# Attention rows stored a tile later, a PSUM bank of rows per engine, list entries made two tiles at a time, and another order behind the last tile

## The chip, the cores and the metric

The kernel runs on one core of a Trainium2 chip. The time is the device time of one execution in microseconds. Before the change it is 892.62 us, the median of 3 runs (892.03 to 894.59). The profile comes from one more execution.

## The reference

Three layers follow one another on 3072 tokens of 512 numbers (4 sequences of 768 steps, 8 heads of 64):

```python
for t in range(S):                       # linear attention with a decay per head
    state = gamma * state + k[t] (x) v[t]
    y[t] = scale * q[t] @ state
logits = x @ w_gate + modality_bias[modality_id]
e_idx  = argmax(logits); gate_w = softmax(logits)[e_idx]
out[e_idx == e] = gate_w * (relu(x @ w1[e]) @ w2[e])      # 8 experts, one for each token
return ((x @ mw1) * (x @ mw2)) @ mw3 @ w_out              # last layer, no activation behind w3
```

Since nothing nonlinear stands between `mw3` and `w_out`, the kernel multiplies these two matrices once ("the fold": 64 units of three 128x512 matmuls) and uses the product for all tokens. Several weights arrive as 64-bit floats, and are decoded on the chip with integer operations ("a decode").

## The kernel before, in words

**Attention.** The tokens go in 24 tiles of 128 (six for each sequence). One Python loop over t writes the program of all engines: in step t the scores of tile t+1 (`scores`, matmuls L331, masked copies on VectorE L333), the output rows of tile t-1 (`rows_gate`, L378), the list entries that are due (`entries`, L447), and tile t itself (`attend_T` L342, `attend_v` L350, `state` L366). Queries, keys and values come as one transposed tile `qkv` (loaded six tiles ahead, seven buffers), a second key tile `kT` (loaded three tiles ahead, four buffers) from tile 6 on; the first six are made on TensorE. Every engine runs its instructions in the order in which this loop writes them, and so do SP's DMA issues. A row tile goes to DRAM (`x_scratch`, L383) where it is made.

**Rows.** `rows_gate(t)` puts the output of a tile and its gate logits, head by head, into one PSUM tile `r` of two banks. ScalarE scales heads 0 to 3 (four instructions, L380), VectorE heads 4 to 7 (L381), and the logits of all heads (`Lh`, L382).

**Routing.** After every batch of tiles (`BATCHES`) VectorE reduces the logits, finds the best expert and its weight (`route_a`), TensorE counts places within experts (`route_mm`, L412 and L414), VectorE finishes (`route_b`). Then each tile gets an entry: VectorE makes a 128x128 one-hot matrix `oh` (L440), TensorE multiplies (L447), ScalarE copies the 16x128 result `ls` (L449), and GpSimd scatters it into a DRAM table `tok_scratch` (L450). The table is filled with a default value at the start (a store of 97x2x256 numbers, L580).

**The two queues.** Routing and entry steps wait in `rq`, decodes in `dq`; at the end of each step `spend(BUDGET)` writes about 2.5 us of VectorE steps from `rq` first, and then from `dq`. `LOAD_T` says after which tiles the loads of the first two 1-MB weights (`f64f`, L189) are written, `SPLIT_T` at which tiles a decode joins `dq`.

**Behind the last tile.** TensorE works off the 64 fold units in pieces (`fold_mm`, lengths in `FM`, matmuls L244, results stored by `fold_out` L261), between them the routing of the last batch, the last entries, the tables of counts, the reading of the lists (`lists_get`, GpSimd, L497), their transposition (`tables3`, L525), the gathers of tokens by list (L793), and the decodes of the last five weights (`fold_a`, `fold_b`). The first expert slot begins with the first matmul of L233 and all slots follow from there to the end.

Of the kernel before, what the change touches and what calls it, by code (L numbers as in the profile page):

```python
# [10 lines left out]
F32 = mybir.dt.float32  # L11
# [83 lines left out]
def pack(q, k, v, moe_modality_id, moe_w_gate, moe_modality_bias, moe_w1, moe_w2, moe2_w1, moe2_w2, moe2_w3, moe2_w_out):  # L95
# [29 lines left out]
    }  # L125
FM = [6, 6, 13, 12, 8, 8]


def kernel(tc, a, out):
# [3 lines left out]
    with ExitStack() as ctx:  # L133
# [45 lines left out]
        pad = ct([1, 1], F32, "pad")  # L179
        lists = fold.tile([P, 2, T2], F32, name="lists")  # L180

# [99 lines left out]
        L = pa.tile([P, NTILE, E], F32, name="L")  # L281
        Lh = pa.tile([P, NTILE, H, E], F32, name="Lh")
        OH = pa.tile([P, NTILE, 2, E], F32, name="OH")
        tmp.append(pa.tile([P, NTILE, E], F32, name="tmp2"))
        none = lists[:TRP]
        io = pa.tile([P, P], F32, name="io_sb")
# [84 lines left out]
        def rows_gate(t):  # L371
            s = st[t]
            xr = pa.tile([P, H, D], F32, tag="xr", name=f"xr{t}", bufs=3)
            b = psr.tile([P, 2, 512], F32, tag="r", name=f"r{t}")[:, :, :4 * HW].rearrange("p x (h w) -> p x h w", h=4)
            g = gx[:, t % NC]
            for hp in range(4):
                z = hp % 2 * 2
                nc.tensor.matmul(b[:, hp // 2, z:z + 2].rearrange("p h w -> p (h w)"), lhsT=s["xT"][:, hp, :], rhs=iwg[:, hp].rearrange("p z w -> p (z w)"), start=True, stop=True)  # L378
            for h in range(4):
                nc.scalar.activation(xr[:, h], b[:, 0, h, :D], AF.Copy, scale=g[:, h:h + 1])  # L380
            V.tensor_tensor(xr[:, 4:], b[:, 1, :, :D], bc(g[:, 4:].unsqueeze(2), [P, 4, D]), op=ALU.mult)  # L381
            V.tensor_tensor(Lh[:, t].rearrange("p (x h) e -> p x h e", x=2), b[:, :, :, D:], bc(g.rearrange("p (x h) -> p x h", x=2).unsqueeze(3), [P, 2, 4, E]), op=ALU.mult)  # L382
            nc.sync.dma_start(xd[t * P:t * P + P, :], xr.rearrange("p h d -> p (h d)"))  # L383
            del st[t]


        def route_a(t0, t1):
            sl, sh = slice(t0, t1), [P, t1 - t0, E]
            V.tensor_reduce(L[:, sl], Lh[:, sl].rearrange("p t h e -> p t e h"), axis=AX.X, op=ALU.add)
# [48 lines left out]
        def places(t):  # L438
            oh = pa.tile([P, P], F32, tag="oh", name=f"oh{t}", bufs=6)
            V.tensor_scalar(oh, io, rk[:, t], None, op0=ALU.is_equal)  # L440
            return oh

        def entries(ohs):
            b = bank()[:2 * E]
            for i, (t, oh) in enumerate(ohs):
                c = slice(i * P, i * P + P)
                nc.tensor.matmul(b[:, c], lhsT=OHV[:, t].rearrange("p z e -> p (z e)"), rhs=oh, start=True, stop=True)  # L447
                ls = pa.tile([2 * E, P], F32, tag="ls", name=f"ls{t}", bufs=4)
                nc.scalar.copy(ls, b[:, c])  # L449
                nc.gpsimd.indirect_dma_start(out=tbl.rearrange("r i -> (r i)").rearrange("(r w) -> r w", w=P), out_offset=bass.IndirectOffsetOnAxis(ap=gix[:, t:t + 1], axis=1), in_=ls, in_offset=None)  # L450

# [14 lines left out]
        gt = CV("gt").rearrange("p (a b) -> p a b", a=E)  # L466

        def tables0():
            c = CV("c16")[:E]
            V.tensor_scalar(nbt, CV("ones")[:E], base[:E, -1:], c, op0=ALU.mult, op1=ALU.subtract)  # L470
# [45 lines left out]
        def tables2b():  # L516
            b = bank()
            for x in range(5):
                nc.tensor.matmul(b[:1, x * CW:x * CW + CW], lhsT=c3[:, x:x + 1], rhs=ident[:, :CW], start=True, stop=True)
            V.tensor_copy(ctl[:, :5 * CW], b[:1, :5 * CW])  # L520

        def tables3():
            b = bank()
            for x in range(2):
                nc.tensor.transpose(b[:, x * P:x * P + P], lists[:, 0, x * P:x * P + P], ident)  # L525
            nc.sync.dma_start(lsd, lists[:NSLOT].rearrange("p z i -> p (z i)"))
            V.tensor_copy(gidx, b[:, :T2].rearrange("p (x j) -> p x j", x=2)[:, :, :NSLOT])

# [17 lines left out]
        nc.gpsimd.memset(Ts[1], 0.0)  # L546
        nc.gpsimd.memset(none[:, 0], float(NT))
        nc.gpsimd.memset(none[:, 1], 0.0)
        nc.gpsimd.memset(iwg[:, :, :, D:], 0.0)
# [81 lines left out]

        def listing(t):
            listed.append((t, places(t)))
            yield .24

# [12 lines left out]
        for t in range(-1, NTILE + 1):  # L648
            for x in {-1: (3, 4, 5)}.get(t, (t + QB - 1,)):
                if x < NTILE:  # L650
                    run(load(x))
            load_k(t + 3)
            if t == 0:
                late_loads()
            if 1 < t + 2 < NTILE and t >= 0:
                vprime(t + 2)
# [44 lines left out]
        def fold_a():  # L701
            if not todo:
                return
            cur.append(fold_split(todo[0], V))
            for _ in range(3):
                next(cur[0])
# [8 lines left out]


        t0, t1 = bounds[-2], bounds[-1]
        while rq:
            spend(99.)
        listed += [(t, places(t)) for t in pend]  # L720
        pend.clear()
        run(routed(t0, t1))
        settle_lists()
        for r in ready:
            route_exp(*r)
        ready.clear()
        fold_mm(FM[0])
        g = settled(t0, t1, route_mm(t0, t1))
        for _ in range(2):
            next(g)  # L730
        bn = tables0()
        finish()
# [642 lines left out]
```

## Time and profile before

| | us |
|---|---|
| median of 3 runs | 892.62 |
| the profiled execution | 891.8 |
| its span on the core | 890.0 |
| TensorE busy | 852.4 (96% of the span) |
| VectorE, ScalarE, GpSimd busy | 485.0, 313.6, 321.3 |
| start of the last rows' entry (L447, tile 16) | 141.16 |
| start of the first expert slot (L233) | 206.36 |

"Busy" counts the time in which an engine runs an instruction; the rest of the span is idle, and the profile names what ended each idle stretch. TensorE's granted clock is given as a share of 2.4 GHz: 1.00 is the upper of its two levels, 0.50 the lower. The share of the DMA is a mean over 16 DMA engines.

### The profile page before, as it was taken

To read this page: it belongs to the slowest core of one execution; us is meant where nothing else is said; L and a number is where in the kernel's file an instruction comes from. 1 tells how busy PE (TensorE), PEld (TensorE's weight loads), DVE (VectorE), ACT (ScalarE), POOL (GpSimd) and SP (SyncE) were. 2 spreads that over 40 slices of the span, in tenths; PEclk is the share of its full clock that TensorE was granted. 3 is DMA by queue.
4 is the path that set the end of the run, shared out by engine and by line. 5 is a ranking of instruction groups with operands and counts; after the bars stand their busy time and mean duration, and the time that the engine had idled before them with its cause. 6 is when DMAs were issued, how large, how long until landed. Compare 5 with 4: busy or idle time off the path is not lost. (4 is left out here: it accounts for less than half of the span.)

```text
span 890.0 us, 16627 instructions
## 1 busy us (share of the span) xinstructions
PE 852.4 (96%) x6363; PEld 770.8 (87%) x6363; DVE 485.0 (54%) x724; ACT 313.6 (35%) x618; POOL 321.3 (36%) x295
## 2 busy tenths in 40 slices
PE   9699997979999999999999998999999999999997
PEld 8598885659999999899999976887887887999997
DVE  2379885755251515661111554256226375999993
ACT  4254442225213131713121442233223253454551
POOL 3223342323003123632200215246326354755663
PEclk9799999999999999999999999999999999999999
DMA  7989842386443526772516019813111414644411
GB/s 276 357 295 315 322 169 85 115 326 217 188 144 144 184 101 204 257 278 93 170 49 253 11 54 386 322 60 142 60 59 48 155 48 154 220 169 145 155 48 60
DMA packets 59334, 152.11 MB, mean 171 GB/s; under 512 B 6775, under 2 KB 20229, under 8 KB 57689
## 3 DMA queue, kind: packets, MB, share of 16 engines
q1 hardware_dynamic: 51321, 127.19, 39.8%
q0 software_dynamic: 7904, 23.53, 7.2%
q8 instruction: 61, 1.00, 0.5%
q14 instruction: 48, 0.39, 0.1%
HBM read 100.98 MB, written 49.75 MB: 169 GB/s over the span
## 5 line engine op out<-in xcount | busy, mean ns | idle before, releaser
L233 PE MATMUL b<-h,wh 128*128 128x256 f32 x768 | 139.9, 284 | 1.1 <-ACT xh L807 1.1
L1007 PE MATMUL al<-xh,ws 128*128 128x512 f32 x384 | 125.4, 394 | 2.0 <-DMA ws<-ws_scratch 1.4
L233 PEld LDWEIGHTS b<-h,wh 128*128 128x128 f32 x768 | 119.7, 192 | 1.7 <-ACT xh L807 1.5
L917 DVE SCALAR_TENSOR_TENSOR h<-b,h 128x512 fp32r<-128x512 f32 x48 | 32.6, 689 | 157.7 <-ACT h L916 157.7
L233 PE MATMUL b<-xh,wl 128*128 128x256 f32 x384 | 108.7, 283 | 0.3 <-DVE wl L204 0.3
L233 PE MATMUL b<-xh,wh 128*128 128x256 f32 x384 | 108.8, 283 | 0.1
L233 PE MATMUL b<-xl,wh 128*128 128x256 f32 x384 | 108.6, 283 | 0.0
L233 PE MATMUL b<-h,wl 128*128 128x256 f32 x384 | 108.6, 283 | 0.0
L1007 PEld LDWEIGHTS al<-xh,ws 128*128 128x128 f32 x384 | 72.0, 188 | 19.5 <-issue 1.7
L1295 PE MATMUL oa<-wfh,ab 128*128 128x256 f32 x384 | 74.9, 284 | 0.7 <-DVE ot L1302 0.6
L1007 PE MATMUL al<-xl,ws 128*128 128x512 f32 x192 | 75.1, 391 | 0.0
L233 PEld LDWEIGHTS b<-xh,wl 128*128 128x128 f32 x384 | 73.7, 192 | 0.5 <-DVE wl L204 0.5
L233 PEld LDWEIGHTS b<-xh,wh 128*128 128x128 f32 x384 | 73.6, 192 | 0.4 <-issue 0.3
L233 PEld LDWEIGHTS b<-xl,wh 128*128 128x128 f32 x384 | 73.7, 192 | 0.0
L233 PEld LDWEIGHTS b<-h,wl 128*128 128x128 f32 x384 | 73.7, 192 | 0.0
L1007 PE MATMUL ga<-xh,ws 128*128 128x512 f32 x192 | 63.6, 392 | 2.3 <-ACT p L1120 1.8
L1295 PEld LDWEIGHTS oa<-wfh,ab 128*128 128x128 f32 x384 | 61.5, 189 | 2.6 <-DVE ot L1302 2.2
L916 ACT ACTIVATE h<-b 128x512 fp32r<-128x512 f32 x48 | 28.4, 597 | 85.2 <-PE b L233 83.7
L952 ACT COPY yT<-b 128x512 f32<-128x512 f32 x24 | 14.1, 588 | 118.5 <-PE b L233 118.5
L1295 PE MATMUL oa<-wfl,ab 128*128 128x256 f32 x192 | 53.8, 280 | 0.0
L204 POOL TENSOR_TENSOR wo<-dec,wo 128x512 fp32r<-128x512 f32 x12 | 16.6, 1394 | 99.2 <-ACT wo L203 99.2
L204 POOL TENSOR_TENSOR xl<-y,xh 128x1024 fp32r<-128x1024 f32 x9 | 21.8, 2425 | 78.5 <-ACT xh L203 78.4
(235 smaller groups left out, 1929.1 us busy)
## 6 DMA issues: line engine op xcount, KB each, us to landing
qkv<-in_qkv SPq DMA_DIRECT2D x22, 768.0 KB
ws_scratch<-wo SPq DMA_DIRECT2D x28, 512.0 KB
ws<-ws_scratch SPq DMA_DIRECT2D x28, 512.0 KB
raw<-in_wall SPq DMA_DIRECT2D x24, 512.0 KB
ab<-ab_scratch SPq DMA_DIRECT2D x24, 512.0 KB
f64f<-in_w SPq DMA_DIRECT2D x8, 1024.0 KB
f64m<-in_m SPq DMA_DIRECT2D x16, 512.0 KB
y_scratch<-yT SPq DMA_DIRECT2D x14, 512.0 KB
```

What stands on the lines that cost most here:

```text
L204: lo_eng.tensor_tensor(lo, src, hi.bitcast(F32), op=ALU.subtract)
L233: nc.tensor.matmul(b, lhsT=x, rhs=y, start=first and n == 0, stop=last and n == 3 * len(ks) - 1)
L916: nc.scalar.activation(h, b, AF.Relu)
L917: V.scalar_tensor_tensor(l, b, 0.0, h.bitcast(F32), op0=ALU.max, op1=ALU.subtract)
L952: nc.scalar.copy(yT[:, 2 * dp:2 * dp + 2, :].rearrange("p a t -> p (a t)"), b)
L1007: nc.tensor.matmul(b, lhsT=y, rhs=r[:, kk, :], start=first and n == 0, stop=n == 5, skip_group_check=True)
L1295: nc.tensor.matmul(b, lhsT=x[:, k], rhs=y[:, k], start=first and n == 0, stop=n == 11, skip_group_check=True)
```

## The change

1. *Stores.* The store of a tile's rows is collected in `stores` and issued by `store_rows()` in the next step, behind that step's loads.
2. *Loads.* `kT` is loaded four tiles ahead into five buffers. The 1-MB loads and the decodes of the loop stand at other tiles. The table's fill is two stores of 97x256.
3. *Rows.* `r` becomes two PSUM tiles, `r0` for ScalarE, `r1` for VectorE. The logits are multiplied in two instructions, the second (heads 0 to 3) written behind `attend_v`. `Lh` keeps two batches.
4. *Entries.* Two tiles at a time: two one-hot matrices, two matmuls, one copy; up to three behind the last tile. The scatters wait in `runs`, and one is issued in each step.
5. *Batches* of 4, 6, 6, 5, 3 tiles in place of 5, 5, 5, 5, 4.
6. *Behind the last tile.* Fold units stand before the last entries, results are stored earlier, a decode's ScalarE copy stands in `fold_a`, one decode moves behind the last weight splits, two copies (`ctl`, `gidx`) go from VectorE to ScalarE, the pieces of `FM` have other lengths, and the rotation of PSUM banks starts the slots at a fixed bank.

```diff
-BATCHES = [5, 5, 5, 5, 4]
-LOAD_T = [0, 2]
-SPLIT_T = [3, 6, 9, 12, 15, 18, 20]
+BATCHES = [4, 6, 6, 5, 3]
+LOAD_T = [1, 3]
+SPLIT_T = [4, 7, 10, 13, 15, 18, 20]
-QB, KB, FB = 7, 4, 5
+QB, KB, FB = 7, 5, 5
-FM = [6, 6, 13, 12, 8, 8]
+FM = [5, 4, 12, 16, 10, 9]
@@ rows_gate
+            gates(t, 1)
+            stores.append((xd[t * P:t * P + P, :], xr.rearrange("p h d -> p (h d)")))
+        def gates(t, x):
+            h, y = slice(4 * x, 4 * x + 4), max(i for i, b in enumerate(bounds) if b <= t)
+            V.tensor_tensor(Lh[:, y % 2, t - bounds[y], h], st[t]["r"][x][:, :, D:], bc(gx[:, t % NC, h].unsqueeze(2), [P, 4, E]), op=ALU.mult)
@@ entries
-                ls = pa.tile([2 * E, P], F32, tag="ls", name=f"ls{t}", bufs=4)
-                nc.scalar.copy(ls, b[:, c])
-                nc.gpsimd.indirect_dma_start(out=tbl..., in_=ls, in_offset=None)
+            ls = pa.tile([2 * E, 3 * P], F32, tag="ls", name=f"ls{ohs[0][0]}", bufs=3)
+            nc.scalar.copy(ls[:, :n], b[:, :n])
+            runs.extend((t, ls[:, i * P:i * P + P]) for i, (t, _) in enumerate(ohs))
@@ the start
-            nc.sync.dma_start(tbl.rearrange("(z r) i -> r z i", z=2), none)
+            for z in range(2):
+                nc.sync.dma_start(tbl[z * TRP:z * TRP + TRP], lists[z][:TRP])
@@ the loop over t
-            load_k(t + 3)
+            load_k(t + 4)
+            store_rows()
             settle()
+            store_run()
                 attend_v(t)
+            if t >= 2:
+                gates(t - 1, 0)
-            if pend:
-                rq.append(listing(pend.pop(0)))
+            if pend and len(runs) + len(listed) < 2:
+                rq.append(listing(pend[:2]))
+                del pend[:2]
@@ behind the last tile
         run(routed(t0, t1))
+        fold_mm(FM[0])
         settle_lists()
+        while runs:
+            store_run()
-        fold_mm(FM[0])
...
+        count_rows()
+        fold_mm(FM[1])
         bn = tables0()
-        fold_mm(FM[1])
+        fold_out()
         settle_lists()
+        while runs:
+            store_run()
         lists_get()
```

Three places show how the instructions move. SP, which issues the loads and stores, from the fill of the table to the load of `kT6`; before:

```order
L580 DMA tok_scratch<-lists_84 97x2x256
L383 DMA x_scratch<-xr0_258 128x512
L189 DMA f64f0_281<-in_wout 128x2048
L300 DMA qkv7_283<-in_qkv 128x1536
L300 DMA qkv8_332<-in_qkv 128x1536
L383 DMA x_scratch<-xr1_362 128x512
L189 DMA f64f1_400<-in_wout 128x2048
L300 DMA qkv9_402<-in_qkv 128x1536
L307 DMA kT6_404<-in_kT 128x512
```

The same place of SP after the change, to the second 1-MB load:

```order
L602 DMA tok_scratch<-lists0_84 97x256
L602 DMA tok_scratch<-lists1_85 97x256
L299 DMA qkv7_284<-in_qkv 128x1536
L388 DMA x_scratch<-xr0_260 128x512
L189 DMA f64f0_334<-in_wout 128x2048
L299 DMA qkv8_336<-in_qkv 128x1536
L306 DMA kT6_338<-in_kT 128x512
L299 DMA qkv9_407<-in_qkv 128x1536
L306 DMA kT7_409<-in_kT 128x512
L388 DMA x_scratch<-xr1_368 128x512
L189 DMA f64f1_473<-in_wout 128x2048
```

`kT6` stands behind four transfers in place of seven, counted from the fill; the second 1-MB load and one `qkv` tile come behind it.

TensorE from the rows of tile 23 on (`r23`; `b` numbers are PSUM banks, `oh` one-hot matrices, `woh`, `wol`, `w3h`, `w3l` halves of the folded weights), before:

```order
L378 MATMUL r23_1782<-iwg_96,xT23_1776 128x144 x4
L447 MATMUL b100_1794<-oh16_1778,OHV_106 16x128
L447 MATMUL b101_1816<-oh17_1799,OHV_106 16x128
L447 MATMUL b101_1816<-oh18_1804,OHV_106 16x128
L447 MATMUL b101_1816<-oh19_1806,OHV_106 16x128
L244 MATMUL b102_1830<-woh0_85,w3h4_1270 128x512
```

The same place after:

```order
L377 MATMUL r23_0_1811<-iwg_97,xT23_1799 128x144 x2
L377 MATMUL r23_1_1812<-iwg_97,xT23_1799 128x144 x2
L458 MATMUL b92_1823<-oh16_1802,OHV_107 16x128
L458 MATMUL b92_1823<-oh17_1804,OHV_107 16x128
L244 MATMUL b93_1845<-woh0_86,w3h4_1282 128x512
L244 MATMUL b93_1845<-wol0_90,w3h4_1282 128x512
```

Before, entries 16 to 19 stand ahead of all fold units, and 20 to 23, the last batch, behind twelve. Now 16 and 17 stand ahead of them, 18 to 20 behind five units, and 21 to 23, the last batch, behind nine.

VectorE in step 8 of the loop (`at` are masked scores, `decf` a decode), before:

```order
L333 TENSOR_TENSOR at9_725<-b35_726,ca_sb_93 128x4x128
L333 TENSOR_TENSOR at9_725<-b36_727,ca_sb_93 128x4x128
L381 TENSOR_TENSOR xr7_738<-r7_739,ca_sb_93 128x256
L382 TENSOR_TENSOR Lh_102<-r7_739,ca_sb_93 128x64
L440 TENSOR_SCALAR oh1_781<-io_sb_105,rk_107 128x128
```

And after:

```order
L332 TENSOR_TENSOR at9_753<-b36_754,ca_sb_94 128x4x128
L332 TENSOR_TENSOR at9_753<-b37_755,ca_sb_94 128x4x128
L380 TENSOR_TENSOR xr7_766<-r7_1_768,ca_sb_94 128x256
L393 TENSOR_TENSOR Lh_103<-r7_1_768,ca_sb_94 128x32
L393 TENSOR_TENSOR Lh_103<-r7_0_767,ca_sb_94 128x32
```

The logits take two instructions, and only the second reads the bank that ScalarE reads too.

## Rows read from the trace of the kernel before

**Rows 1.** Windows of four stages: length, busy by engine, clock, DMA share, GB/s.

```profile
35.30:45.50 10.20, 4.92 (x28) 4.70 (x29) 1.65 (x4) 0.59 (x3) 0.00 (x0) 0.50 0.75 301
45.50:141.20 95.70, 92.54 (x1175) 80.20 (x1174) 80.03 (x177) 46.44 (x149) 32.70 (x32) 1.00 0.74 261
141.20:206.40 65.20, 54.01 (x242) 40.40 (x242) 39.77 (x87) 16.46 (x31) 16.78 (x16) 0.95 0.52 183
206.40:890.00 683.60, 670.31 (x4548) 617.32 (x4546) 350.55 (x434) 233.60 (x395) 259.02 (x225) 1.00 0.41 148
```

**Rows 2.** Timeline of TensorE, tiles 6 and 7: start, us, line [idle before].

```profile
28.45 1.16 PE L331 MATMUL b<-qkv,kT 64*128 64x128 f32 x16
...
31.61 1.09 PE L350 MATMUL b<-at,vp 128*64 128x128 f32 x16
40.58 2.08 PE L331 MATMUL b<-qkv,kT 64*128 64x128 f32 x16 [7.87 <-DMA kT<-in_kT]
...
46.05 1.09 PE L350 MATMUL b<-at,vp 128*64 128x128 f32 x16
```

**Rows 3.** The timeline of SP's DMA issues, the table's fill and kT6.

```profile
13.41 0.26 SPq L580 DMA_DIRECT2D tok_scratch<-lists  x1
...
27.53 0.33 SPq L307 DMA_DIRECT2D kT<-in_kT  x1
```

**Rows 4.** Waits: engine, line, waited for, total us, times, longest.

```profile
SPq L307 <- DMA tok_scratch<-lists: 2.2, 1, 2.2
DVE xr L381 <- ACT xr L380: 17.6, 15, 3.7
```

**Rows 5.** The windows view, three shorter stretches.

```profile
21.00:22.00 1.00, 1.00 (x11) 0.88 (x12) 0.00 (x0) 0.86 (x4) 0.78 (x3) 1.00 0.07 24
27.50:40.50 13.00, 5.20 (x76) 4.65 (x70) 5.00 (x9) 3.78 (x9) 3.02 (x2) 0.80 1.02 411
50.00:100.00 50.00, 49.46 (x648) 43.29 (x648) 43.29 (x97) 25.18 (x81) 16.80 (x16) 1.00 0.93 333
```

**Rows 6.** The timeline of GpSimd, the scatters and the reading of the lists.

```profile
122.86 0.87 POOL L450 DMA_INDIRECT tok_scratch<-ls,gix  x1 [0.79 <-PE b L350]
...
129.76 0.87 POOL L450 DMA_INDIRECT tok_scratch<-ls,gix  x1 [4.96 <-DMA tok_scratch<-ls,gix]
...
142.59 0.84 POOL L450 DMA_INDIRECT tok_scratch<-ls,gix  x1 [3.58 <-ACT ls L449]
148.06 0.84 POOL L450 DMA_INDIRECT tok_scratch<-ls,gix  x1 [4.62 <-DMA tok_scratch<-ls,gix]
150.78 0.84 POOL L450 DMA_INDIRECT tok_scratch<-ls,gix  x1 [1.88 <-DMA tok_scratch<-ls,gix]
...
169.41 1.45 POOL L450 DMA_INDIRECT tok_scratch<-ls,gix  x1 [1.85 <-DMA tok_scratch<-ls,gix]
172.74 1.01 POOL L497 DMA_INDIRECT lists<-tok_scratch,ridx  x1 [1.88 <-DVE decf L198]
```

**Rows 7.** Waits of SP, 141 to 207 us.

```profile
SPq L775 <- DMA tok_scratch<-ls,gix: 1.7, 1, 1.7
```

**Rows 8.** The timeline of SP, the load of a late 1-MB weight.

```profile
174.43 0.54 SPq L189 DMA_DIRECT2D f64f<-in_w  x1
```

**Rows 9.** The timeline of VectorE, the last decodes.

```profile
186.86 0.69 DVE L194 TENSOR_SCALAR decf<-f64f 128x1024 uint32<-128x1024 uint32 x1 [4.86 <-DMA f64f<-in_w]
...
193.13 2.59 DVE L204 TENSOR_TENSOR wl<-raw,wh 128x1024 fp32r<-128x1024 f32 x1 [0.73 <-ACT wh L203]
```

**Rows 10.** The timeline of TensorE behind the last tile.

```profile
141.16 0.39 PE L447 MATMUL b<-oh,OHV 128*16 128x128 f32 x2
...
191.20 0.50 PE L244 MATMUL b<-woh,w3h 128*128 128x512 f32 x1 [3.04 <-ACT w3h L217]
...
206.36 0.28 PE L233 MATMUL b<-xh,wh 128*128 128x256 f32 x1
```

**Rows 11.** Groups by line of VectorE, 46 to 141 us: busy, mean ns, idle.

```profile
L382 DVE TENSOR_TENSOR Lh<-r,ca_sb 128x64 f32<-128x64 f32 x19 | 4.0, 213 | 0.0
```

More of the change, by code (lines that the diff above doesn't have):

```diff
@@ L179 @@
         pad = ct([1, 1], F32, "pad")
-        lists = fold.tile([P, 2, T2], F32, name="lists")
+        lists = [fold.tile([P, T2], F32, name=f"lists{z}") for z in range(2)]
         woh = [fold.tile([P, 1024], F32R, name=f"woh{i}") for i in range(4)]
@@ L281 @@
         L = pa.tile([P, NTILE, E], F32, name="L")
-        Lh = pa.tile([P, NTILE, H, E], F32, name="Lh")
+        Lh = pa.tile([P, 2, max(BATCHES), H, E], F32, name="Lh")
         OH = pa.tile([P, NTILE, 2, E], F32, name="OH")
         tmp.append(pa.tile([P, NTILE, E], F32, name="tmp2"))
-        none = lists[:TRP]
         io = pa.tile([P, P], F32, name="io_sb")
@@ L373, in rows_gate @@
             xr = pa.tile([P, H, D], F32, tag="xr", name=f"xr{t}", bufs=3)
-            b = psr.tile([P, 2, 512], F32, tag="r", name=f"r{t}")[:, :, :4 * HW].rearrange("p x (h w) -> p x h w", h=4)
+            s["r"] = b = [psr.tile([P, 512], F32, tag=f"r{x}", name=f"r{t}_{x}")[:, :4 * HW].rearrange("p (h w) -> p h w", h=4) for x in range(2)]
             g = gx[:, t % NC]
@@ L377, in rows_gate, with store_rows @@
                 z = hp % 2 * 2
-                nc.tensor.matmul(b[:, hp // 2, z:z + 2].rearrange("p h w -> p (h w)"), lhsT=s["xT"][:, hp, :], rhs=iwg[:, hp].rearrange("p z w -> p (z w)"), start=True, stop=True)
+                nc.tensor.matmul(b[hp // 2][:, z:z + 2].rearrange("p h w -> p (h w)"), lhsT=s["xT"][:, hp, :], rhs=iwg[:, hp].rearrange("p z w -> p (z w)"), start=True, stop=True)
             for h in range(4):
[L380 to L384, printed above, removed]
+                nc.scalar.activation(xr[:, h], b[0][:, h, :D], AF.Copy, scale=g[:, h:h + 1])
+            V.tensor_tensor(xr[:, 4:], b[1][:, :, :D], bc(g[:, 4:].unsqueeze(2), [P, 4, D]), op=ALU.mult)
+            gates(t, 1)
+            stores.append((xd[t * P:t * P + P, :], xr.rearrange("p h d -> p (h d)")))
+        stores = []
+        def store_rows():
+            for y, x in stores:
+                nc.sync.dma_start(y, x)
+            stores.clear()
+        def gates(t, x):
+            h, y = slice(4 * x, 4 * x + 4), max(i for i, b in enumerate(bounds) if b <= t)
+            V.tensor_tensor(Lh[:, y % 2, t - bounds[y], h], st[t]["r"][x][:, :, D:], bc(gx[:, t % NC, h].unsqueeze(2), [P, 4, E]), op=ALU.mult)
+            if not x:
+                del st[t]
         def route_a(t0, t1):
             sl, sh = slice(t0, t1), [P, t1 - t0, E]
-            V.tensor_reduce(L[:, sl], Lh[:, sl].rearrange("p t h e -> p t e h"), axis=AX.X, op=ALU.add)
+            V.tensor_reduce(L[:, sl], Lh[:, bounds.index(t0) % 2, :t1 - t0].rearrange("p t h e -> p t e h"), axis=AX.X, op=ALU.add)
             yield
@@ L438, in places @@
         def places(t):
-            oh = pa.tile([P, P], F32, tag="oh", name=f"oh{t}", bufs=6)
+            oh = pa.tile([P, P], F32, tag="oh", name=f"oh{t}", bufs=4)
             V.tensor_scalar(oh, io, rk[:, t], None, op0=ALU.is_equal)
@@ L524, in tables3 @@
             for x in range(2):
-                nc.tensor.transpose(b[:, x * P:x * P + P], lists[:, 0, x * P:x * P + P], ident)
-            nc.sync.dma_start(lsd, lists[:NSLOT].rearrange("p z i -> p (z i)"))
-            V.tensor_copy(gidx, b[:, :T2].rearrange("p (x j) -> p x j", x=2)[:, :, :NSLOT])
+                nc.tensor.transpose(b[:, x * P:x * P + P], lists[0][:, x * P:x * P + P], ident)
+            for z in range(2):
+                nc.sync.dma_start(lsd[:, z * T2:z * T2 + T2], lists[z][:NSLOT])
+            nc.scalar.copy(gidx, b[:, :T2].rearrange("p (x j) -> p x j", x=2)[:, :, :NSLOT])
         def tables4():
@@ L546 @@
         nc.gpsimd.memset(Ts[1], 0.0)
-        nc.gpsimd.memset(none[:, 0], float(NT))
-        nc.gpsimd.memset(none[:, 1], 0.0)
+        for z in range(2):
+            nc.gpsimd.memset(lists[z][:TRP], float(NT) * (1 - z))
         nc.gpsimd.memset(iwg[:, :, :, D:], 0.0)
@@ L579, in late_loads @@
             nc.sync.dma_start(io, a["io"])
-            nc.sync.dma_start(tbl.rearrange("(z r) i -> r z i", z=2), none)
+            for z in range(2):
+                nc.sync.dma_start(tbl[z * TRP:z * TRP + TRP], lists[z][:TRP])
         def biases():
@@ L630, in spend, with listing @@
                     us -= c
-        def listing(t):
-            listed.append((t, places(t)))
-            yield .24
+        def listing(ts):
+            for t in ts:
+                listed.append((t, places(t)))
+                yield .24
         def settle_lists():
@@ L704, in fold_a @@
             cur.append(fold_split(todo[0], V))
-            for _ in range(3):
+            for _ in range(4):
                 next(cur[0])
@@ L747 @@
         pss += [(ps2, f"b{i}") for i in range(5, 7)]
+        count[0] += (4 - count[0]) % 7
         ar = [ctx.enter_context(tc.tile_pool(name="ar1", bufs=1, side="left"))]
```

26 lines of the change are left out of this document (17 added, 9 removed).

## The prediction, made before the changed kernel ran

> **What bounds the kernel now.** First the busy times: TensorE works in 852.4 of 890.0 us, so without fewer matmuls only 37.6 us of idle can be won, and what runs at the lower clock. Second the windows by stage, to see where the idle lies [rows 1]: 13.3 us in the slots (683.60 - 670.31), which the change hardly touches, 11.2 behind the last tile (65.20 - 54.01), only 3.2 in 95.7 us of the loop. Third the timeline of TensorE for single gaps: one of 7.87 us stands before the scores of tile 6 and ends with the load of `kT` [rows 2]. The reader is to see there that the work behind the gap is slow, too: from the scores (L331) to the values (L350) it takes 5.47 us (46.05 - 40.58), one tile earlier 3.16 (31.61 - 28.45), and the granted clock is 0.50 from 35.3 to 45.5 us [rows 1, 2]. So this place costs 7.9 + 2.3 = 10.2 us.
>
> Why that load is late takes three more views. SP issues the table's fill at 13.41 and `kT6` only at 27.53 [rows 3]; the waits name the fill as what this issue waited for [rows 4]; and while only the fill moves, the DMA share is 0.07 at 24 GB/s, about one engine of 16 [rows 5]. From 27.5 to 40.5 the engines are full (1.02, 411 GB/s). My reading: the fill lies on one DMA engine for 14 us, that engine's part of everything issued meanwhile queues behind it, and a transfer lands with its last part. In SP's order eight transfers run from the fill's successor to `kT6`; by their shapes 0.25 + 1 + 0.75 + 0.75 + 0.25 + 1 + 0.75 + 0.25 = 5.0 MB. At 411 GB/s that is 12.8 us (5.24 million bytes), from 27.5 to 40.3; the scores begin at 40.58.
>
> Behind the last tile I read GpSimd first. A scatter waits for the landing of the one before: eight of them take from 142.59 to 169.41, then the lists are read (172.74) [rows 6]. SP's raw expert weights also wait for that last scatter [rows 7], behind them is a 1-MB load issued at 174.43 [rows 8], VectorE waits 4.86 us for it until 186.86 [rows 9], and TensorE 3.04 us for its decode until 191.20. The first slot starts at 206.36 [rows 10]. So this stage hangs on the scatters, not on its 54 us of matmuls.
>
> **The start.** `kT6` now has only 0.75 + 0.25 + 1 + 0.75 + 0.25 = 3.0 MB from the fill to its own end. At the same rate that is 7.7 us from 27.5 on: 35.2. The scores want it at 32.7 (31.61 + 1.09, end of the row before) [rows 2]. The gap becomes 2.5 us: 5.4 gained. The lower clock began 2.6 us into the old gap (35.3 - 32.7), so the new one is at the edge: of the 2.3 us I count 1.0 as still lost, 1.3 gained. What is late next: `kT8` stands behind 3.25 MB more than `kT6`, 8.3 us, so it lands near 43.5, and two tiles of 4.2 us (32.7 - 28.45) after 35.2 its scores come at 43.6. I take off 0.7. Sum 6.0. Bounds: 0 if the load lands as before, 10.2 if it is never late.
>
> What the row shows is one busy engine while one store of 97 rows moves; on which engines two of them lie, no row of before shows. The Trainium skill ("DMA: Bandwidth & Descriptors", "Why a DMA increments its semaphore by 16 and not by 1") says that a transfer uses the largest number up to 16 that divides its slowest dimensions; for 97 rows, a prime, one, so each of the two stores would be on one engine. The trace agrees for the one store (0.07 against 1/16). By that rule, with both on the same engine, the new order brings the 6.0; with two engines sharing the work it would be the 10.2 of the first rival.
>
> **The loop.** A single entry is a 0.39-us row of TensorE with a switch on either side [rows 10]. Of the 16 singles eight pairs are left; a pair can save between 0 and one such row, 3.1 in all; I take half, 1.6, since only the switch is certain. Of 3.2 us of idle [rows 1] some ends on one-hot matrices and goes to the pairs: 0.8, between 0 and 3.2. Against it stands VectorE: one logit product of 213 ns becomes two [rows 11]; the second costs between 0 and 213 ns, 0 to 5.1 us for 24 tiles. VectorE has 6.71 us free in 50 [rows 5], 12.8 in the loop, so the sum fits; what is bunched (pairs, decodes closer at the end) I charge with 0.9. Net 1.5, between -4 and +6. The product that waits for ScalarE has the routing and decode steps behind it, and then the next masked scores, for which TensorE waits; before, the wait stood on `xr` (17.6 us in 15 times) [rows 4], so it moves and does not grow. The stores a tile later delay only gathers 40 us on; a scatter per step stands beside 1-us products on GpSimd, which is idle mostly (32.70 busy of 95.70) [rows 1]: both nothing, and with that cover gone a scatter costs what rival D says.
>
> **Behind the last tile.** Eight scatters (16 to 23) remain. The first can start 1.6 us after the last rows (before 142.59 - 141.16 = 1.4, now one copy for two). A quiet cycle is 2.72 us (150.78 - 148.06), one with a 1-MB load beside it 5.47 (148.06 - 142.59) [rows 6]. All entries are made early enough, 18 to 20 behind five fold units, 21 to 23 behind nine, so the scatters follow one another: 1.6 + 7 x 2.72, one of them longer by 2.75 = 23.4, and 3.33 to the reading of the lists (172.74 - 169.41) = 26.7 us after 141.16. Before: 31.58. Gain 4.9. From there to 191.20 the same chain, 18.5 us. Of the last 15.2 (206.36 - 191.20) a 2.59-us product of VectorE (L204 at 193.13) [rows 9] now stands before the decode; TensorE meets its result two thirds of the way, 1.9 gained. Two copies on ScalarE, idle for 49 of 65 us [rows 1], cost nothing. Sum 6.8; bounds 11.2 (all idle) [rows 1] and rival D below. The bank rotation in the slots meets no bank that anything waits for: 0, at most 1 either way.
>
> **Sum.** 891.8 (the profiled execution; span 890.0 and 1.8 around it) - 6.0 - 1.5 - 6.8 = 877.5; the median of the runs lies 0.8 above that execution: 878.3.
>
> **Rivals.**
> A, the start is free: the two stores share two DMA engines, or SP issues `kT6` early enough. For: SP no longer waits for the fill at this issue if eight transfers may be open, since more of them lie between. Against: the queue on the engine is the same. 878.3 - 4.2 = 874.1.
> B, the tail gives back: the raw weights and lists take their time behind earlier scatters, the clock falls in a new gap (it was 0.95 in this stage) [rows 1]. For: three chains end close together. Tail gain 0: 885.1.
> C, the stall stays as it was: the load still queues until 40. For: the fill has the same bytes. 878.3 + 6.0 = 884.3. The change would then not do at the start what its order says.
> D, slower: the scatters run at the longest cycle of the trace, 6.9 us (129.76 - 122.86) [rows 6], because the last 1-MB loads are now issued among them. 1.6 + 7 x 6.9 + 3.33 = 53.2, 21.6 later than before: 891.8 - 6.0 - 1.5 + 21.6 - 1.9 + 0.8 = 904.8. It decides from a cycle at which the loss reaches 9.4 (6.0 + 1.5 + 1.9): (31.6 + 9.4 - 4.9) / 7 = 5.2 us. Against: of seven cycles behind the last tile the mean is 3.83 ((169.41 - 142.59) / 7).
> E, VectorE sets the loop: 43.29 of 50 us, with 12 more products of 213 ns and half the present wait on `xr` (17.6 / 15 / 2 = 0.6) for each of 12 tiles, is 53: 6% more, 5.7 us of the loop in place of 1.5 gained: 885.5.
>
> **Chances.** Forecast 0.50, A 0.15, B 0.13, C 0.08, E 0.07, D 0.07. The forecast's own range is 874 to 882. With A, B, C and E within it the range is 869 (A with 5 us more from the tail) to 888. About 0.3%, 2.7 us, is what can be told from no change. Faster: all but D and a part of E, 0.90; within 0.3%: 0.04, the edge of B, E and D; slower 0.06.
>
> **What would show it.** The gap before tile 6's scores at 2 to 3 us and the clock hardly at 0.50 there (A: no gap; C: 7 to 8). Loop from tile 7 to the last rows shorter by 1 to 2 us. Reading of the lists 26 to 28 us after the last rows, first slot 57 to 60 (before 65.2). It is wrong if scatters wait for entries or for 1-MB loads more than once, if VectorE's one-hot products end TensorE's gaps in the loop, or if the slots take longer than 683.6.

## The result, and the profile after

The changed kernel takes 881.56 us (median of 4 runs, 877.44 to 883.86) against 892.33 (4 runs, 892.01 to 894.59): the ratio is 0.987, with an interval of 0.983 to 0.991. The forecast was 878.3 with a range of 869 to 888. The profiled execution is the longest of the four, 883.86 us with a span of 882.1.

The windows of the changed kernel, cut where its stages end (columns as in [rows 1]):

```profile
34.97:131.32 96.35, 93.44 (x1202) 82.86 (x1202) 86.49 (x199) 48.82 (x146) 31.34 (x32) 1.00 0.83 305
131.32:160.94 29.62, 29.57 (x148) 22.95 (x147) 22.00 (x70) 5.43 (x12) 9.87 (x9) 1.00 0.16 57
160.94:172.05 11.11, 0.01 (x2) 0.00 (x1) 0.00 (x0) 0.00 (x0) 2.83 (x3) 0.66 0.56 165
172.05:178.30 6.25, 6.25 (x16) 4.98 (x17) 2.52 (x3) 4.10 (x6) 3.68 (x4) 0.52 1.04 428
198.70:882.10 683.40, 670.14 (x4548) 617.40 (x4546) 349.51 (x434) 233.66 (x395) 259.08 (x225) 1.00 0.41 148
```

The loop of this profile has no low clock any more, and the slots take 683.4 us as before (683.6). Behind the last tile 29.6 us are packed without a gap, then TensorE stands still for 11.1 us, and afterwards runs at the low clock. Its timeline shows what ended the gaps:

```profile
33.00 1.09 PE L349 MATMUL b<-at,vp 128*64 128x128 f32 x16
34.97 1.16 PE L330 MATMUL b<-qkv,kT 64*128 64x128 f32 x16 [0.88 <-DMA kT<-in_kT]
...
38.78 1.09 PE L349 MATMUL b<-at,vp 128*64 128x128 f32 x16
...
172.05 0.69 PE L545 MATMUL b<-cb_sb,lists 128*128 128x128 f32 x2 [11.10 <-DMA lists<-tok_scratch,ridx]
...
184.99 0.79 PE L244 MATMUL b<-woh,w3h 128*128 128x512 f32 x1 [2.15 <-ACT w3h L217]
...
198.70 0.28 PE L233 MATMUL b<-xh,wh 128*128 128x256 f32 x1
```

Tile 6's scores start at 34.97 and not at 40.58, and the work behind them takes 3.81 us (38.78 - 34.97, with 0.55 us of routing matmuls in it) and not 5.47 [rows 2]. The last rows end at 131.4 (before 141.2), so 9.8 us are won up to there; 5.6 at tile 6 and 4.2 behind it, of which 2.3 is the clock. But the first slot starts 67.3 us after the last rows, before 65.1: this stage gave 2.2 back. 5.6 + 4.2 - 2.2 + 0.3 (slots) = 7.9 = 890.0 - 882.1.

GpSimd's timeline answers to [rows 6]:

```profile
145.52 1.78 POOL L469 DMA_INDIRECT tok_scratch<-ls,gix  x1 [1.37 <-DMA tok_scratch<-ls,gix]
151.97 1.21 POOL L469 DMA_INDIRECT tok_scratch<-ls,gix  x1 [4.68 <-DMA tok_scratch<-ls,gix]
155.06 1.82 POOL L469 DMA_INDIRECT tok_scratch<-ls,gix  x1 [1.88 <-ACT w3h L217]
159.96 0.84 POOL L469 DMA_INDIRECT tok_scratch<-ls,gix  x1 [3.08 <-DMA tok_scratch<-ls,gix]
...
164.90 1.01 POOL L517 DMA_INDIRECT lists<-tok_scratch,ridx  x1 [1.88 <-DMA tok_scratch<-ls,gix]
```

Two cycles are long (6.45 and 4.90 us), and the lists are read 33.5 us after the last rows, against 31.5 before and 26.7 in the forecast. Only beside the first of the two does SP issue a 1-MB load (at 146.60 us); in the second the DMA share is at most 0.04.

### The profile page after: what moved, and what is told of

Same layout as the page of the kernel before. It is cut to its first block, busy times and chain, and to the rows that moved or that the text cites. A ratio compares the mean times of both kernels' runs of the same rounds, so it can differ in the third digit from the quotient of the medians.

```text
span 882.1 us, 16621 instructions
## 1 busy us (share of the span) xinstructions
PE 849.6 (96%) x6363; PEld 771.9 (88%) x6363; DVE 487.6 (55%) x746; ACT 313.8 (36%) x607; POOL 321.6 (36%) x295
## 5 line engine op out<-in xcount | busy, mean ns | idle before, releaser
L990 ACT COPY yT<-b 128x512 f32<-128x512 f32 x24 | 14.1, 587 | 118.8 <-PE b L233 118.8
L204 POOL TENSOR_TENSOR wo<-dec,wo 128x512 fp32r<-128x512 f32 x12 | 16.5, 1391 | 99.5 <-ACT wo L203 99.5
L469 POOL DMA_INDIRECT tok_scratch<-ls,gix x24 | 24.5, 1020 | 77.0 <-DMA tok_scratch<-ls,gix 33.4
```

Of the source, the lines that this page charges most:

```text
L204: lo_eng.tensor_tensor(lo, src, hi.bitcast(F32), op=ALU.subtract)
L990: nc.scalar.copy(yT[:, 2 * dp:2 * dp + 2, :].rearrange("p a t -> p (a t)"), b)
```

## The experiments

Where the time is won or lost is read from four marks in each profile: the start of tile 6's scores, the end of the last rows, the first reading of the lists, and the first slot. Each ratio is to runs of the kernel before that were taken together with the experiment (their medians are 891.69 to 893.35 us).

| kernel | tile 6 at | to last rows | to lists | to slot | median us | ratio to before, interval |
|---|---|---|---|---|---|---|
| before | 40.58 | 100.66 | 31.50 | 33.63 | 892.33 | |
| changed | 34.97 | 96.42 | 33.51 | 33.79 | 881.56 | 0.987 (0.983 to 0.991) |
| changed_again | 34.55 | 99.45 | 26.07 | 37.94 | 880.54 | 0.986 (0.983 to 0.990) |
| start_alone | 34.73 | 98.44 | 32.37 | 34.01 | 884.34 | 0.989 (0.986 to 0.993) |
| fill_96 | 35.69 | 100.92 | 32.76 | 33.66 | 886.68 | 0.994 (0.992 to 0.996) |
| old_tail | 34.84 | 96.86 | 29.31 | 32.74 | 879.43 | 0.984 (0.981 to 0.988) |
| x10_first | 34.83 | 96.05 | 28.82 | 34.49 | 880.14 | 0.986 (0.983 to 0.989) |
| one_r_tile | 34.36 | 98.00 | 29.44 | 33.89 | 882.65 | one run |
| singles | 35.01 | 97.50 | 27.09 | 35.05 | 881.57 | 0.988 (0.984 to 0.992) |
| drain | 35.41 | 114.70 | 25.88 | 35.51 | 893.76 | 1.001 (0.999 to 1.003) |
| loads_first | 35.02 | 95.99 | 28.09 | 45.73 | 893.49 | 1.002 (1.001 to 1.004) |
| loads_spread | 35.26 | 97.37 | 29.03 | 23.92 | 868.54 | 0.972 (0.969 to 0.975) |
| spread_fill96 | 33.51 | 96.24 | 33.88 | 24.51 | 872.29 | 0.975 (0.970 to 0.979) |

**start_alone.**

```diff
-LOAD_T = [0, 2]
+LOAD_T = [1, 3]
-SPLIT_T = [3, 6, 9, 12, 15, 18, 20]
+SPLIT_T = [4, 7, 10, 13, 15, 18, 20]
-QB, KB, FB = 7, 4, 5
+QB, KB, FB = 7, 5, 5
...
-            load_k(t + 3)
+            load_k(t + 4)
...
+            store_rows()
...
-            nc.sync.dma_start(tbl.rearrange("(z r) i -> r z i", z=2), none)
+            for z in range(2):
+                nc.sync.dma_start(tbl[z * TRP:z * TRP + TRP], none[:, z])
```

> The kernel before with the change's start alone: loads and decodes of the loop at the new tiles, kT four tiles ahead in five buffers, rows stored a tile later, the fill as two stores (to make room, four one-hot buffers for six and three entry buffers for four). My theory (the late kT6 is the start's whole cost, and its landing follows the megabytes ahead of it): the gap before tile 6's scores falls from 7.9 to between 0.5 and 2.6 us, the clock there stays at 1.00, about 8 us gained, 882 to 886. Rival (the shorter gap of the changed kernel owes to its split row banks or its pairs): the gap stays above 5 us and the time above 889.

Tile 6's scores and the rows behind them in its timeline of TensorE, and one of its windows:

```profile
34.73 1.16 PE L331 MATMUL b<-qkv,kT 64*128 64x128 f32 x16 [1.65 <-DMA kT<-in_kT]
35.82 2.12 PE L378 MATMUL r<-iwg,xT 128*128 128x144 f32 x8
37.73 1.88 PE L342 MATMUL b<-qkv,T 128*128 128x128 f32 x8
39.54 1.09 PE L350 MATMUL b<-at,vp 128*64 128x128 f32 x16
```

```profile
36.00:38.00 2.00, 2.00 (x10) 2.00 (x11) 1.76 (x3) 0.00 (x0) 0.00 (x0) 0.51 1.00 410
```

The gap is 1.65 us and the time 884.34, both as the theory said. Its clock did not come: the scores still run at full speed (1.16 us), but the rows behind them take 2.12 and 1.88 us (1.25 and 1.16 in the changed kernel) at a granted clock of 0.51. From the scores to the values it takes 4.81 us (39.54 - 34.73), one tile at the full clock 3.16 [rows 2], so 1.65 of the 2.3 us are still lost here. Even so the start alone is most of the change's gain (891.69 - 884.34 = 7.4 us).

**fill_96.**

```diff
-            nc.sync.dma_start(tbl.rearrange("(z r) i -> r z i", z=2), none)
+            to = tbl.rearrange("(z r) i -> r z i", z=2)
+            for r in (slice(0, TR), slice(TR, TRP)):      # TR = 96, TRP = 97
+                nc.sync.dma_start(to[r], none[r])
```

> The kernel before; only the table's fill of 97 rows is issued as 96 rows and then 1 row, nothing else moves. Theory (a store of 97 rows lies on one of 16 DMA engines and holds up everything behind it; 96 rows spread over all): the DMA share from 21 to 22 us is no longer 0.07, SP's issue of kT6 no longer waits for the fill, kT6 lands some 5 us sooner, gap 0.5 to 3 us, time 883 to 887. Rival (kT6 is late for the 5 MB ahead of it, whichever engines the fill uses): gap above 6 us, time within 2 us of before.

Its windows from 15 and from 21 us, and its row of tile 6's scores:

```profile
15.00:16.00 1.00, 1.00 (x20) 0.97 (x16) 0.54 (x2) 0.98 (x5) 0.00 (x0) 1.00 1.00 393
21.00:22.00 1.00, 1.00 (x11) 1.00 (x10) 0.54 (x1) 0.60 (x2) 0.78 (x3) 1.00 0.95 369
```

```profile
35.69 1.18 PE L331 MATMUL b<-qkv,kT 64*128 64x128 f32 x16 [2.29 <-DMA kT<-in_kT]
```

With nothing changed but the shape of one store the DMA share goes from 0.07 [rows 5] to 0.95, the gap from 7.87 to 2.29, and 5.0 us are won between the medians (891.69 and 886.68). So the late `kT6` hung on the store of 97 rows, as the forecast read it. How it did so is not split up: SP also issues `kT6` 3.0 us sooner here (at 24.57, before at 27.53 [rows 3]), so the wait of SP for that store and the queue on its DMA engine are both in these 5 us. The clock falls behind this gap, too: the step of tile 6 takes 6.26 us (4.65 for the step of tile 8, at the full clock), so 1.6 us are lost.

**changed_again** is the changed kernel once more.

> The changed kernel itself once more, for a second profile of it. Theory (its first profile had a run of slow scatters by chance, 33.5 us from the last rows to the reading of the lists, where three kernels with the same code up to there had 28.8 to 29.4): 28 to 31 us, first slot 62 to 65 us after the last rows, time 879 to 882. Rival (the 33.5 is the rule): 32 us or more again, time 882 or more.

The list reading came at 26.1 us, earlier than the theory's 28 to 31, the slot at 64.0, the time is 880.5. So the 33.5 was not the rule, but one profile is no measure of this stage: over seven profiles with the new scatters (this one, the changed kernel's first, x10_first, one_r_tile and the three with moved loads) it is 26.1 to 33.9, in the mean 29.8; in the three that have the scatters of before 31.5 to 32.8, in the mean 32.2. What the earlier lists won was not kept: behind them this profile takes 37.9 us to the slot, the first one 33.8. Its rows of GpSimd, VectorE and TensorE:

```profile
160.07 1.66 POOL L517 DMA_INDIRECT lists<-tok_scratch,ridx  x1 [1.88 <-DVE decf L194]
```

```profile
174.13 4.02 DVE L204 TENSOR_TENSOR wl<-raw,wh 128x1024 fp32r<-128x1024 f32 x1 [2.85 <-DMA xg<-x_scratch,gidx]
178.07 0.68 DVE L194 TENSOR_SCALAR decf<-f64f 128x1024 uint32<-128x1024 uint32 x1
```

```profile
182.40 0.50 PE L244 MATMUL b<-woh,w3h 128*128 128x512 f32 x1 [4.13 <-ACT w3h L217]
```

The decode of the tenth weight (178.07) stands behind a split of a raw weight and starts 18.0 us after the list reading, before the change 14.1 (186.86 - 172.74) [rows 6, 9].

**old_tail** takes the changed kernel with the lines behind the loop from before:

```diff
-FM = [5, 4, 12, 16, 10, 9]
+FM = [6, 6, 13, 12, 8, 8]
         run(routed(t0, t1))
-        fold_mm(FM[0])
         settle_lists()
+        fold_mm(FM[0])
...
-            nc.scalar.copy(gidx, b[:, :T2]...)
+            V.tensor_copy(gidx, b[:, :T2]...)
```

> The changed kernel with everything behind the last tile in the order of before (pieces of 6, 6, 13, 12, 8 and 8 units, entries ahead of the fold units, the two copies on VectorE). Theory (this stage hangs on the scatters and what follows them, not on where the fold units stand; two scatters more are still open at the last tile than before): the lists are read 32 to 35 us after the last rows, the first slot starts 65 to 69 us after them, time within 3 us of the changed kernel. Rival (the new order made the single idle stretch of 11 us and the low clock behind it, and costs 4 us): first slot 61 to 64 us after the last rows, time 876 to 879.

The slot comes 62.05 us after the last rows, as the rival had it, the time, 879.4, is within the theory's 3 us, and the list reading at 29.3 is in neither's numbers. What separates this profile from the changed kernel's is the list reading; behind it the two orders take 32.74 and 33.79 us (37.94 in changed_again). So the new order was worth nothing that can be measured here.

**x10_first.**

```diff
+        fold_a()
+        fold_b()
         split_w(3)
         split_w(0)
         raw_load(expert(e0), range(4, 8))
         fold_mm(FM[4])
-        fold_a()
-        fold_b()
         split_w(1)
```

> The changed kernel; only the decode of the tenth weight stands ahead of the splits of the raw weights (split_w 3 and 0) again, as before the change. Theory (in the changed kernel VectorE takes the split first, waits for raw weights there, and then decodes beside GpSimd's split, so that the tenth decode comes 4 us after its load): the decode starts within 1 us of its load's landing, the first slot starts 61 to 64 us after the last rows (67.3 in the changed kernel's profile), time 876 to 879. Rival (the 11-us gap and the low clock behind it are what costs): the first slot stays at 66 us or later, time 880 or more.

VectorE in the changed kernel, then in x10_first (L204 splits a raw weight, L194 begins a decode):

```profile
177.01 1.23 DVE L204 TENSOR_TENSOR wl<-raw,wh 128x1024 fp32r<-128x1024 f32 x1 [1.84 <-DMA wf_scratch<-wfo]
178.15 0.69 DVE L194 TENSOR_SCALAR decf<-f64f 128x1024 uint32<-128x1024 uint32 x1
178.87 3.73 DVE L196 SCALAR_TENSOR_TENSOR decf<-f64f,decf 128x1024 uint32<-128x1024 uint32 x1
```

```profile
172.44 0.74 DVE L194 TENSOR_SCALAR decf<-f64f 128x1024 uint32<-128x1024 uint32 x1 [2.62 <-DMA f64f<-in_w]
...
178.77 3.75 DVE L204 TENSOR_TENSOR wl<-raw,wh 128x1024 fp32r<-128x1024 f32 x2 [0.73 <-DMA xg<-x_scratch,gidx]
182.45 0.68 DVE L194 TENSOR_SCALAR decf<-f64f 128x1024 uint32<-128x1024 uint32 x1
```

The decode of the tenth weight does start when its load lands, 12.7 us after the list reading in place of 13.2, and the splits (3.75 us) then stand before the eleventh decode. The slot comes 63.3 us after the last rows, inside the theory's 61 to 64, but because the lists were read at 28.8 and not at 33.5 us: from the list reading to the slot it is 34.49 us, between the changed kernel's 33.79 and 37.94. The time, 880.14, is above the theory's 876 to 879 and cannot be told from the changed kernel's (881.56 and 880.54). So it is not borne out that the swapped decode costs 4 us: what one decode wins the next one loses.

**loads_first** and **loads_spread.** Both write the decodes of the last weights, and with them the last 1-MB loads, ahead of the raw loads; the second puts eight fold units behind each decode:

```diff
         fold_mm(FM[2])
         tables2b()
+        fold_a()
+        fold_b()
+        fold_mm(8)
+        fold_a()
+        fold_b()
         e0 = load_ctl(1, 0, 1, E - 1, SP)[0]
         raw_load(expert(e0), range(4))
+        fold_mm(8)
         fold_a()
         fold_b()
         fold_mm(FM[3])
         tables3()
...
```

> The changed kernel with the decodes of the last weights written before the raw expert weights, so that the last two 1-MB loads no longer stand on SP behind the raw loads, which wait for the last scatter; the units of the fold follow without a break (pieces of 5, 4, 12, 27, 8, 6). Theory (the chain is last scatter, raw loads, 1-MB load, decode, last 16 fold units): both loads are issued before 165 us, TensorE has done all 64 units by 185, the first slot starts 50 to 60 us after the last rows (67.4 in the changed kernel's profile), time 868 to 876, though the scatters beside the loads may cost 3 to 6 us more. Rival (lists and gathers end the stage, not the weights): the first slot at 64 us or later, time 878 or more.

> As loads_first, but with each decode followed by eight fold units, so that no copy of a fold result stands on ScalarE behind a cast that waits for a decode. Theory (loads_first lost because TensorE waited 14.6 us for a bank whose copy stood behind the casts, not because the loads came early): no gap above 4 us behind the last tile, all 64 units done by 182 us, the first slot 48 to 56 us after the last rows, time 864 to 872. Rival (the lists and gathers set the end): first slot at 60 us or later, time 875 or more.

loads_first, TensorE, then ScalarE (L217 casts a decoded weight, L260 copies a fold result out of its bank):

```profile
171.81 0.80 PE L244 MATMUL b<-woh,w3h 128*128 128x512 f32 x1 [14.57 <-ACT wfo L260]
...
185.53 0.38 PE L545 MATMUL b<-cb_sb,lists 128*128 128x128 f32 x2
```

```profile
164.59 1.04 ACT L217 CAST w3h<-decf 128x1024 fp32r<-128x1024 f32 x1 [4.54 <-DVE decf L198]
170.23 1.04 ACT L217 CAST w3h<-decf 128x1024 fp32r<-128x1024 f32 x1 [4.59 <-DVE decf L198]
171.18 0.58 ACT L260 COPY wfo<-b 128x512 f32<-128x512 f32 x1
```

The loads were early, the edit was not: the copy that frees a bank stood behind a cast that waited for the last decode, and TensorE, and behind it the lists, waited 14.6 us. With the copies between the casts, in loads_spread, SP and TensorE show:

```profile
160.56 0.33 SPq L189 DMA_DIRECT2D f64f<-in_w  x1
162.16 1.82 SPq L813 DMA_DIRECT2D raw<-in_wall  x4
```

```profile
169.82 0.41 PE L545 MATMUL b<-cb_sb,lists 128*128 128x128 f32 x2 [2.21 <-DMA lists<-tok_scratch,ridx]
...
185.57 0.28 PE L233 MATMUL b<-xh,wh 128*128 128x256 f32 x1
```

All 1-MB loads are issued before the raw loads, TensorE waits once, for 2.2 us, and the slot follows the list reading by 23.9 us in place of 33.8, 52.9 us after the last rows, as the theory said. 868.54 us is 13 us less than the changed kernel, and the lowest median of all. So the stage hung on the chain from the last scatter over raw loads, last 1-MB loads and decodes to the last fold units, and taking the loads out of it wins 10 us. Loads, decodes and fold units move together in this edit; what each is worth by itself is not shown.

**spread_fill96** adds the 96 + 1 rows of fill_96 to it:

```diff
             for z in range(2):
-                nc.sync.dma_start(tbl[z * TRP:z * TRP + TRP], lists[z][:TRP])
+                nc.sync.dma_start(tbl[z * TRP:z * TRP + TR], lists[z][:TR])
+            for z in range(2):
+                nc.sync.dma_start(tbl[z * TRP + TR:z * TRP + TRP], lists[z][TR:TRP])
```

> The kernel of loads_spread with each half of the table's fill issued as 96 rows and 1 row. Theory (what is left of the gap before tile 6 is the fill on one DMA engine): the gap of 1.4 us goes to under 0.4, everything else as loads_spread, time 865.5 to 868.5. Rival (the 3 MB ahead of kT6 hold it up by themselves): gap 1 us or more, time as loads_spread, 868 to 870.

```profile
32.48 1.09 PE L349 MATMUL b<-at,vp 128*64 128x128 f32 x16
33.51 1.16 PE L330 MATMUL b<-qkv,kT 64*128 64x128 f32 x16
```

In this row of TensorE the gap is gone. The time is not lower for that (872.29 in six runs from 862.8 to 873.5; loads_spread 868.54 in four from 866.3 to 872.4): in the profiled execution the list reading came 33.9 us after the rows, and 6.5 us of idle stand there. The mechanism is shown, a gain in time is not.

**drain.**

```diff
             settle()
-            store_run()
+            while runs:
+                store_run()
```

> The changed kernel, with all waiting scatters written in a step of the loop and not one. Theory (scatters left over by one per step put the list reading some 3 us later): 8 scatters after the last rows in place of 9, the lists read 29 to 31 us after the last rows (33.5 in the changed kernel's profile), time 1 to 4 us less, 878 to 880. Rival (each scatter waits for the landing of the one before anyway, so that the order of writing changes nothing): the lists read at 33 us or later, time as the changed kernel.

TensorE, and GpSimd around the same place:

```profile
117.08 1.12 PE L365 MATMUL acc<-vp,qkv 128*64 128x64 f32 x16 [9.47 <-POOL vp L311]
```

```profile
109.62 0.88 POOL L469 DMA_INDIRECT tok_scratch<-ls,gix  x1 [3.16 <-DMA tok_scratch<-ls,gix]
115.12 0.84 POOL L469 DMA_INDIRECT tok_scratch<-ls,gix  x1 [4.61 <-DMA tok_scratch<-ls,gix]
115.98 3.04 POOL L311 TENSOR_TENSOR vp<-qkv,ca_sb 128x512 f32<-128x512 f32 x3
```

The lists are read 25.9 us after the last rows, earlier than the theory's 29 to 31, but the loop takes 18.3 us more, and the time, 893.76, is far from its 878 to 880. Two gaps of 4.09 and 9.47 us are 13.6 of the 18.3; most of the rest is the clock behind gaps (TensorE is busy for 99.3 in place of 93.5 us, at a mean clock of 0.91). A second scatter in a step waits on GpSimd for the landing of the first, the products `vp` stand behind it, and TensorE behind them. One scatter a step is what keeps this wait short. It is not nothing there either: in changed_again the same row of TensorE waits 2.15 us, and the matmuls behind it run slower (1.62 us for the scores that take 1.16; the clock is 0.50 from 112 to 114 us):

```profile
110.18 0.69 PE L365 MATMUL acc<-vp,qkv 128*64 128x64 f32 x16 [2.15 <-POOL vp L311]
110.79 1.62 PE L330 MATMUL b<-qkv,kT 64*128 64x128 f32 x16
```

**one_r_tile** and **singles** undo one part of the loop each: the two PSUM tiles of a tile's rows, and the pairs (`pend[:1]` for `pend[:2]`; behind the loop at most three entries share a copy).

```diff
-            s["r"] = b = [psr.tile([P, 512], F32, tag=f"r{x}", ...) for x in range(2)]
+            rt2 = psr.tile([P, 2, 512], F32, tag="r", name=f"r{t}")
+            s["r"] = b = [rt2[:, x, :4 * HW].rearrange("p (h w) -> p h w", h=4) for x in range(2)]
```

```diff
-                rq.append(listing(pend[:2]))
-                del pend[:2]
+                rq.append(listing(pend[:1]))
+                del pend[:1]
```

> The changed kernel with the rows of a tile in one PSUM tile of two banks again; the two instructions for the logits stay. Theory (the wait of VectorE only moves from the rows to the logits, so the split is worth little): from tile 6's scores to the last rows 96 to 97.5 us (96.4 in the changed kernel's profile). Rival (the split is what made the loop shorter): 98 us or more.

> The changed kernel with the list entries of the loop made for one tile at a time again. Theory (pairs save switches of TensorE and waits for one-hot matrices): from tile 6's scores to the last rows 97.5 to 99 us (95.9 to 96.5 in kernels with pairs), 1 to 2 us slower than the changed kernel. Rival (the loop is shorter for the split rows alone): 96 to 97 us, same time.

The loop takes 98.0 and 97.5 us, the latter just inside what the pairs' theory said, the former at the rival's edge. But kernels with the changed loop itself go from 96.0 to 99.45 from profile to profile, and singles and changed_again have the same time within their intervals (881.57 and 880.54). TensorE's busy time between the same two marks (the first number behind the stretch and its length) says more; start_alone, one_r_tile and singles:

```profile
34.73:133.17 98.44, 96.56 (x1201) 83.98 (x1202) 80.15 (x181) 47.88 (x152) 33.82 (x32) 0.98 0.79 287
34.36:132.36 98.00, 93.94 (x1203) 83.12 (x1204) 85.20 (x202) 48.16 (x144) 31.90 (x32) 1.00 0.82 298
35.01:132.52 97.51, 95.02 (x1201) 82.41 (x1202) 86.91 (x197) 48.34 (x154) 33.14 (x32) 1.00 0.80 299
```

In the six profiles that have the whole new loop at the full clock it is 93.2 to 93.5 us. Without the pairs it is 1.6 us more (95.0), as in start_alone when its 1.65 us of low clock are taken off (94.9); without the split banks 0.6 more (93.9). So the pairs take 1.6 us off TensorE's work. That either part shortens the kernel's time is not shown: the idle in the loop differs by more than that between profiles (2.6 to 4.2 us with the new loop).

## Why the prediction was right, and where it was wrong

**The start: right, with two terms too cautious.** The sum said 6.0: 5.4 from the gap, 1.3 of 2.3 from the clock, 0.7 taken off for `kT8`. The landing of `kT6` was to be 35.2 and was 34.97; the scores were ready later than before (34.09, not 32.7), so the gap was 0.88. The clock stayed at 1.00, so all 2.3 came back, and no gap shows at tile 8: 7.9 in the profile. In start_alone's profile, with a gap of 1.65 us, it is 5.9 and 0.7 of the clock, 6.5. That the landing was hit within 0.3 us is in part luck: the sum counts the megabytes from 27.5 us on, but the DMA share is 0.79 or more from 23 us on, in the kernel before and in the changed one, so the engines were busy some 4 us earlier than the sum has them.

Rival A did not come: with both stores of 97 rows the DMA share at 21 us was 0.07 in start_alone as in before (the changed kernel's first profile has 0.07 from 20 us and 0.13 from 21, the kernel before 0.13 and 0.07), and the gap is gone only with 96 + 1 rows in the new order (spread_fill96). That is the engine count by which the Trainium skill ("DMA: Bandwidth & Descriptors", the section named in the prediction) sends 97 rows to one engine and 96 to sixteen; the windows of fill_96 agree. Rival C is excluded by the gap.

**The loop: the work as forecast, the rest not shown.** 1.5 was forecast: 1.6 for the rows that pairs save, 0.8 of idle won, 0.9 lost to VectorE. The 1.6 came, in TensorE's busy time (singles). The other two terms cannot be told from the spread: with the low clock at tile 6 taken off, the loop takes 98.3 us before, 96.8 in start_alone and 99.3 in fill_96, 98.1 in the mean; the seven profiles with the new loop unaltered (changed, changed_again, old_tail, x10_first and the three with moved loads) have 96.0 to 99.45, in the mean 96.9. The scatter in each step, put at nothing, cost 0.3 us of waiting in the first profile, and 2.15 and a stretch at the low clock in changed_again, whose loop is the longest of the seven. Rival E did not come: VectorE is busy for 86.5 of 96.4 us, and its products for the logits end one gap of 0.98 us.

**Behind the last tile: wrong.** 6.8 were forecast; the two profiles of the changed kernel have 67.3 and 64.0 us in place of 65.1, so between 2.2 lost and 1.1 gained. Two steps failed.

"The scatters follow one another", with one cycle prolonged, came in the second profile: eight scatters, one long cycle of 6.1 us, the lists at 26.1 us against 26.7. In the first, nine scatters were still to be issued, the first of them 4.0 us after the last rows and not 1.6, and two cycles were long; in the mean over kernels the list reading moved by 2.4, not 4.9. Rival D did not come: the mean cycle is 3.5 us (131.02 to 162.18, nine cycles).

"From there the same chain, 18.5 us" failed in both. From the list reading to TensorE's first matmul with the tenth weight it takes 20.1 us (184.99 - 164.90) and 22.3 (182.40 - 160.07), and from there to the slot 13.7 and 15.6 in place of 15.2, so 1.5 gained and 0.4 lost in place of 1.9 gained. I took two stages that overlap for one that adds up, and moved a split ahead of a decode that was itself on the path: in changed_again that decode starts 18.0 us after the lists and not 14.1, in the first profile at 13.2, but one of its instructions takes 3.73 us in place of 1.23. "Two copies on ScalarE cost nothing" is doubtful as well. ScalarE in the changed kernel's first profile:

```profile
172.77 0.19 ACT L548 CAST gidx<-b 128x38 int32<-128x38 f32 x1 [17.49 <-PE b L545]
172.86 1.05 ACT L217 CAST w3h<-decf 128x1024 fp32r<-128x1024 f32 x1
```

The copy waits there for the lists, and the cast of a weight whose decode is done waits behind it; VectorE waits 14.6 us for that cast. Whether this reaches the slot is not shown; old_tail, which has the copies on VectorE, has the same time.

The clock was left out, too, but what it cost is smaller than it looks. In the first profile the fold units are gone 11 us before the lists come (4.4 in the second), and 16 matmuls behind that gap run at 0.52; at 0.43 us from one matmul to the next in place of 0.23 the 14 fold matmuls there cost 2.9 us. But behind them TensorE waits 2.15 us for a decode, so no row shows that these 2.9 reach the slot. 7 matmuls at 185 us cost another 1.4, and the kernel before ran at 0.54 at this place, too (192 to 195 us). Rival B had 0.13; in size, for this stage alone, it was the case that came.

**The sum.** 6.0 + 1.5 + 6.8 = 14.3 were forecast, 10.8 came (892.33 - 881.56). That it lies inside the likeliest case's own range of 874 to 882 is partly luck: up to 2 more at the start stand against 6 to 9 less behind the last tile.

## What to carry to other kernels

Look at the number of rows of a store before asking why later loads are late: one awkward row count made the load of `kT6` 5 us late, and 96 + 1 rows in place of 97 took these 5 us out by one line. Where a stage ends with a chain of loads, order the issues by what waits longest behind them, and keep the copies that free a bank out from behind casts that wait for a load; here that was worth 13 us, more than the whole change. Packing work ahead of a wait moves the idle, it does not remove it (old_tail and the changed kernel have the same time), and the work behind one long gap runs at the low clock.

## What the runs showed of the hardware

- A store of 97 rows kept the DMA share at 0.07; 96 rows and 1 row brought it to 0.95, and with them the load of `kT6` ended TensorE's wait 4.9 us sooner (35.69 and 40.58).
- Behind the last rows of the changed kernel's two profiles a scatter of 16 rows follows the one before it, for which it waits, after 2.2 to 3.1 us, with a 1-MB load issued in between after 6.1 and 6.5; one cycle took 4.9 us without a load beside it. From one execution of the same program to the next the list reading moved by 7 us (26.1 and 33.5).
- Gaps of 0.9 to 1.5 us before tile 6's scores left the granted clock at 1.00 (eight profiles). Behind gaps of 1.65, 2.29, 2.63 and 7.87 us (start_alone, fill_96, drain, before) it was about 0.50 for a while, which cost 1.6 to 2.3 us.
- A VectorE step of 1.23 us took 3.73 us (L196 at 178.87, above) while GpSimd split a weight (179.10, 2.41 us), and in changed_again a split of 1.23 us took 4.02 (L204 at 174.13; GpSimd from 174.65, 2.40 us).
